# Attention scores of two heads in one pass over row halves of the array

## The chip, the cores and the metric

One core of one Trainium2 chip runs the whole kernel. The metric is device time in microseconds of one execution; lower is better. TensorE does matrix products into PSUM banks, VectorE (DVE) and ScalarE (ACT) read PSUM, GpSimd (POOL) works on SBUF, and SyncE (SP) issues most DMAs. The five run side by side and wait for each other by semaphores; each works through its own instructions in the order in which the program issues them.

## The reference

Three stages follow each other: attention with hashed buckets, a mixture of experts, and a mixing stage. The change touches the first one alone, for 2 batches of 8 heads, 768 positions, 64 dimensions:

```python
q_bits = (einsum('bhsd,dk->bhsk', q, proj) > 0)      # 6 bits; k_bits likewise
mask = q_bucket[:, :, :, None] == k_bucket[:, :, None, :]
scores = where(mask, q @ k.T / sqrt(64), -1e9)
attn = exp(scores - max(scores)); attn /= sum(attn) + 1e-9
out = attn @ v
```

## The kernel before

Heads are taken in 8 pairs (2 batches of 4), with the 64 dimensions of the two heads of a pair above each other in the 128 partitions. A pair has two halves of 384 queries, a half three blocks of 128, and each block a unit for each head: 96 units `u`, 6 to a group `g`, 16 groups. In what follows a pair of units is the two heads of one query block, 48 in all.

Single-precision products come from two halves of each number: a high part rounded to fp32r and the rest, a low part. A score is the sum of high x high, high x low and low x high. The bucket test is an addition too: 12 rows of bits (each bit and its complement, the keys' scaled by a huge number) add a penalty wherever a bit differs.

For each pair of heads, GpSimd makes the high and low parts (`split_hi`, `split_lo`) in the tile `hl`, and DMAs on SP's queue (`place`) lay them out anew in the operand tile `op`: for each head, 128 rows hold q high twice over k high and k low, and 76 rows hold q low and 12 rows of bits. A unit's scores (`scores`, L198) are then four matmuls over 128 columns of queries, one 128-row and one 76-row product for each half of 384 keys. They go to a buffer `ps` of two PSUM banks; there are two such buffers.

What follows a unit's scores:

- `low` (L205): one VectorE instruction takes the row minimum (signs are turned) and moves the 768 scores out of PSUM into `sc`;
- `expo` (L212): ScalarE's exponential with the row sum;
- `transp` (L226 to L232): six TensorE transposes through two banks `pst`, copied out by ScalarE or VectorE; three copies in four are ScalarE's;
- `av` (L243): attention times values in two column halves of the array, one for each head, four matmuls after every odd unit, each of which the chip runs as two instructions; `av_out` takes the result out after six;
- `av_tok` (L260 to L275): once in a group, the product with the identity and gate weights, and its small VectorE steps.

The order is written out by hand. The main loop runs over units: scores of unit u + 2, `av` after odd units, transposes of u (which also issue `low` and `expo` of u + 2), then a list of side jobs that `at` has put down for this unit: splits and placing for the next pair of heads, bits (`bit_part`: the dots of L118 on TensorE in four column groups, signs on VectorE, a GpSimd multiply), loads, and `narrow`, the conversion of 64-bit weights for the third stage (a load, three VectorE steps, L528 to L532, and a store). The first pair of heads is prepared by hand ahead of the loop: copies on ScalarE and GpSimd make head 0's operands (L424 to L431), VectorE its bits, and DMAs head 1's; six warm-up matmuls stand between. The first six units go head by head.

Of the kernel before, what the change touches and what calls it, by code (L numbers as in the profile page):

```python
# [27 lines left out]
NW = 4  # L28
C_ID, C_TRI, C_ONE = 0, 128, 256
# [29 lines left out]
def attention(tc, nc, cst, cbf, cst_src, tri_src, cw, qkT, vt, iw_src, route, wide, errands, xh, early):  # L59
    with ExitStack() as ctx:  # L60
# [24 lines left out]
        rawt, vtile, bits, opnd, hls = {}, {}, {}, {}, {}  # L85

        def load_pair(i):
            b, p = pairs[i]
            r = raw_p.tile([128, 2, S], F32, name="rqk")
            if i == 0:  # L90
                nc.sync.dma_start(r[:, 1], qkT[b, p, :, 1])
                nc.sync.dma_start(r[:, 0], qkT[b, p, :, 0])
            else:
                nc.sync.dma_start(r, qkT[b, p])
            rawt[i] = r
# [36 lines left out]
        def bits_here(s, hf, pd):  # L132
            sl, p = slice(384 * hf, 384 * hf + 384), 64 * s
            to = opnd[0][64:76, 0, 2 + s, sl]
            nc.vector.tensor_scalar(to, pd[p:p + 12, :384], 0.0, cw[p:p + 12, 32:33],
                                    op0=ALU.is_gt, op1=ALU.subtract)
            return to

        def split_hi(i, j):
            raw = rawt[i]  # L140
            if j == 0:
                hls[i] = hl_p.tile([128, 4, S], F32R, name="hl")
                if i == 0:
                    nc.scalar.activation(hls[i][:, 2], raw[:, 1], AF.Copy)
                else:
                    nc.gpsimd.tensor_scalar(hls[i][:, 2], raw[:, 1], 1.0, 0.0, op0=ALU.mult, op1=ALU.add)
            elif i == 0:
                nc.scalar.activation(hls[i][:, 0], raw[:, 0], AF.Copy, scale=-0.125)
            else:
                nc.gpsimd.tensor_scalar(raw[:, 0], raw[:, 0], -0.125, 0.0, op0=ALU.mult, op1=ALU.add)  # L150
                nc.gpsimd.tensor_scalar(hls[i][:, 0], raw[:, 0], 1.0, 0.0, op0=ALU.mult, op1=ALU.add)

        def split_lo(i, j):
            raw, hl = rawt[i], hls[i]
            if j == 0:
                eng = nc.gpsimd if i else nc.vector
                eng.tensor_tensor(hl[:, 3], raw[:, 1], hl[:, 2].bitcast(F32), op=ALU.subtract)
            elif i == 0:
                nc.vector.scalar_tensor_tensor(hl[:, 1], raw[:, 0], -0.125, hl[:, 0].bitcast(F32),
                                               op0=ALU.mult, op1=ALU.subtract)  # L160
            else:
                nc.gpsimd.tensor_tensor(hl[:, 1], raw[:, 0], hl[:, 0].bitcast(F32), op=ALU.subtract)

        def place(i, h, j):
            if i not in opnd:
                opnd[i] = op_p.tile([128, 2, 4, S], F32R, name="op")
            o32, h32 = opnd[i].bitcast(F32), hls[i].bitcast(F32)
            bt, r0 = bits[i]
            hs = slice(64 * h, 64 * h + 64)
            if j == 0:  # L170
                nc.sync.dma_start(o32[0:64, h, 1:4:2], h32[hs, 2:3].to_broadcast([64, 2, S]))
            elif j == 1:
                nc.sync.dma_start(o32[64:128, h, 0:2], h32[hs, 0:4:3])
            elif j == 2:
                nc.sync.dma_start(o32[0:64, h, 0:4:2], h32[hs, 0:2])
            else:
                for s in range(2):
                    c = r0 + 64 * s + 12 * h
                    nc.sync.dma_start(o32[64:76, h, 2 + s], bt[c:c + 12])

        units = [(i, half, qb, h) for i in range(NPR) for half in range(2) for qb in range(3) for h in range(2)]
        units[:6] = sorted(units[:6], key=lambda t: (t[3], t[2]))
# [4 lines left out]
        def scores(u):  # L187
            i, half, qb, h = units[u]
            op = opnd[i]
            g = u // 6  # L190
            if u % 6 == 0:
                sums[g] = sm_p.tile([128, 6], F32, name="sum")
                mns[g] = sm_p.tile([128, 6], F32, name="mn")
            ps = ps_s.tile([128, 2, 512], F32, name="ps")
# [5 lines left out]
            pss[u] = ps  # L200
# [14 lines left out]
        def transp(u):  # L215
# [6 lines left out]
            for n in range(2):  # L222
# [10 lines left out]
                if n == 0 and u + 2 < NU:  # L233
                    low(u + 2)
            if u + 2 < NU:
                expo(u + 2)
# [9 lines left out]
        def av_out(g, q0=0, q1=3):  # L246
            if q0 == 0:
                xTs[g] = sm_p.tile([128, 384], F32, name="xT", bufs=2)
# [44 lines left out]
        def cut(x, p0, m, eng):  # L293
            if not xcut:
                t = op_p.tile([128, 2, 4, S], F32R, name="op").rearrange("p a b s -> p (a b s)")
                for h in range(2):
                    xcut[h] = t[:, 3072 * h:3072 * h + 3072].rearrange("p (a t d) -> p a t d", a=2, t=3)
# [8 lines left out]
        def pick(ks):  # L306
            if not hot:
                t = op_p.tile([128, 2, 4, S], F32R, name="op").rearrange("p a b s -> p (a b s)")
# [27 lines left out]
        def narrow(m, j):  # L336
            src, dst = wide[m]
            if j == 0:
                w64[m] = d_p.tile([128, S], U32, name="w64", bufs=3)
# [16 lines left out]
        busy, relieve = set(), set(range(1, NU - 1, 2))  # L356
        for n in range(1, NPR):
            u0 = 12 * (n - 1)
            u1 = u0 + 3 if n == 1 else u0
            at(u1, split_hi, n, 0)  # L360
            at(u1, split_hi, n, 1)
            at(u1 + 1, split_lo, n, 0)
            at(u1 + 2, split_lo, n, 1)
            for h in range(2):
                for j in range(4):
                    at(u1 + 3 + j, place, n, h, j)
# [4 lines left out]
        for u0, ids in ((1, [1]), (9, [2, 3]), (26, [4, 5]), (50, [6, 7])):  # L371
            for hf in range(2):
                at(u0 + hf, lambda ids=ids, hf=hf: bit_part(ids, hf, px_tile))
                busy.add(u0 + hf)
# [3 lines left out]
        for m in range(len(wide)):  # L378
            for j in range(1, 4):
                x = free.pop(0)  # L380
                at(x, narrow, m, j)
                if j == 1 and m + 2 < len(wide):
                    at(x, narrow, m + 2, 0)
            at(x + 1, narrow, m, 4)
        for x, f in enumerate(errands):
# [4 lines left out]
        for x, f in zip((0, 1, 3, 4, 5, 6, 7, 8, 9), [copy] + seg):  # L390
# [4 lines left out]
        tok[70], tok[71] = [8], [9]  # L395
# [19 lines left out]
        idle = ps_a.tile([128, 512], F32, name="pav")  # L415
        warm(nc, cbf, idle, 13)
        opnd[0] = op_p.tile([128, 2, 4, S], F32R, name="op")
        op = opnd[0]
        split_hi(0, 0)
        hl = hls[0]  # L420
        split_lo(0, 0)
        split_hi(0, 1)
        for x in (1, 3):
            nc.gpsimd.tensor_scalar(op[0:64, 0, x], hl[0:64, 2], 1.0, 0.0, op0=ALU.mult, op1=ALU.add)  # L424
        pds = [bit_dots([0], hf, pt_tile) for hf in range(2)]
        warm(nc, cbf, idle, 6)
        split_lo(0, 1)
        nc.scalar.activation(op[0:64, 0, 0], hl[0:64, 0], AF.Copy)
        nc.scalar.activation(op[64:128, 0, 1], hl[0:64, 3], AF.Copy)
        nc.scalar.activation(op[64:128, 0, 0], hl[0:64, 0], AF.Copy)  # L430
        nc.scalar.activation(op[0:64, 0, 2], hl[0:64, 1], AF.Copy)  # L431
        k0 = bits_here(1, 0, pds[0])
        bits_here(0, 0, pds[0])
        nc.vector.tensor_scalar(k0, k0.bitcast(F32), -MISS, None, op0=ALU.mult)
        k1 = bits_here(1, 1, pds[1])
        nc.vector.tensor_scalar(k1, k1.bitcast(F32), -MISS, None, op0=ALU.mult)
        place(0, 1, 0)
        place(0, 1, 1)
        place(0, 1, 2)
        for hf in range(2):  # L440
            bit_signs(bits[0][0], hf, pds[hf])
        place(0, 1, 3)
        nc.sync.dma_start(op.bitcast(F32)[64:76, 0, 2, 384:], bits[0][0][0:12, 384:])
        nc.sync.dma_start(iw, iw_src)
        nc.sync.dma_start(tri, tri_src)
        load_v(0)
        load_pair(2)
        load_v(1)
        load_pair(3)
        for u in range(2):  # L450
            scores(u)
            low(u)
            expo(u)
        nc.gpsimd.tensor_copy(cbf[:, 0:128], ident)
        nc.gpsimd.tensor_copy(cbf[:, 128:384], tri)
        for u in range(NU):
            g, w = u // 6, u % 6
            last = g == NG - 1
            if u + 2 < NU:
                scores(u + 2)  # L460
            if g >= 1 and not last and w % 2 == 1:
                av(g - 1, w - 1)
                av(g - 1, w)
            if w == 5 and g >= 1 and not last:
                av_out(g - 1)
            if last and w == 1:
                for kb in range(3, NB):
# [1005 lines left out]
```

## Time and profile before

| | us |
|---|---|
| median of 3 runs | 641.53 |
| the runs | 638.04, 642.39, 641.53 |
| the profiled execution | 639.75 |
| span of its instructions | 637.9 |

| engine | busy in the span | share |
|---|---|---|
| TensorE | 621.0 | 97% |
| VectorE | 404.0 | 63% |
| ScalarE | 355.3 | 56% |
| GpSimd | 262.0 | 41% |

The profiled execution is 1.85 us longer than the span from its first to its last instruction; the rest lies around it. Busy shares are means over three stages; attention fills the first 250 us or so. TensorE counts as busy from the start of a matmul to its modelled end, and neighbours overlap, so the durations of single matmuls don't add up to the time that a stream takes.

### The profile page before, as it was taken

The numbers are of one execution on the slowest core, as the hardware profiler recorded it, in microseconds if no ns is written. First come the engines' busy times: TensorE is split into PE (matmuls) and PEld (weight loads), VectorE is DVE, ScalarE is ACT, GpSimd is POOL, SyncE is SP. The second block draws the span as 40 slices with busy tenths as digits, with TensorE's granted clock in tenths as the row PEclk, the third lists the DMA queues.
The fourth block names the chain that finished last, engine by engine and source line by source line (L and its number), as shares of the span: only waits on it lengthen the run. The fifth ranks groups of instructions, "written<-read, shape, count | busy, mean of one in ns | idle before, by whom it ended". The sixth has DMA issues, their size and how long they took to land. (4 is left out here: it accounts for less than half of the span.)

```text
span 637.9 us, 10353 instructions
## 1 busy us (share of the span) xinstructions
PE 621.0 (97%) x3930; PEld 501.9 (79%) x3930; DVE 404.0 (63%) x743; ACT 355.3 (56%) x645; POOL 262.0 (41%) x195
## 2 busy tenths in 40 slices
PE   7989998999999999999999999999999999999997
PEld 4746766667677677889899889989688887878897
DVE  6636768788888666846885655644356877663352
ACT  5747766767767766454555455444656546743220
POOL 2432221124080241345346354255456766684320
PEclk8979999999999999999999999999999999999999
DMA  7997999965976201688768698764222432221002
GB/s 198 265 234 203 305 260 289 260 165 159 259 219 157 74 1 50 232 294 316 272 226 312 233 308 306 256 247 168 82 85 85 145 100 84 101 97 67 33 34 100
DMA packets 52861, 116.13 MB, mean 182 GB/s; under 512 B 4180, under 2 KB 13664, under 8 KB 52808
## 3 DMA queue, kind: packets, MB, share of 16 engines
q1 hardware_dynamic: 49448, 101.28, 51.2%
q10 hardware_dynamic: 1440, 7.86, 3.6%
q0 software_dynamic: 1920, 6.29, 3.0%
q8 instruction: 32, 0.52, 0.3%
q14 instruction: 21, 0.17, 0.1%
HBM read 74.06 MB, written 22.54 MB: 151 GB/s over the span
## 5 line engine op out<-in xcount | busy, mean ns | idle before, releaser
L205 DVE TENSOR_SCALAR_CACHE_REDUCE sc<-ps 128x768 f32<-128x768 f32 x96 | 91.4, 953 | 33.2 <-PE ps L198 32.2
L1199 PE MATMUL acc<-wt,z 128*128 128x256 f32 (+1 forms) x576 | 105.4, 338 | 0.6 <-DVE z L1185 0.6
L1199 PEld LDWEIGHTS acc<-wt,z 128*128 128x128 f32 x576 | 89.8, 188 | 15.7 <-DVE z L1185 1.5
L784 POOL TENSOR_TENSOR whl<-wr,whl 128x1024 fp32r<-128x1024 f32 x30 | 72.0, 2425 | 69.6 <-ACT whl L782 69.6
L212 ACT ACTIVATE sc<-sc,mn 128x768 f32<-128x768 f32 x96 | 89.8, 936 | 18.6 <-DVE sc L205 15.4
L198 PE MATMUL ps<-op 76*128 76x384 f32 (+1 forms) x384 | 94.2, 367 | 4.8 <-DMA op<-bt 2.2
L857 PE MATMUL mph<-xhl,whl 128*128 128x256 f32 x768 | 94.2, 284 | 0.4 <-DVE xhl L520 0.3
L857 PEld LDWEIGHTS mph<-xhl,whl 128*128 128x128 f32 x768 | 93.2, 192 | 1.3 <-DVE xhl L520 0.5
L226 PEld LDWEIGHTS pst<-cst,sc 128*128 128x128 f32 x576 | 66.5, 143 | 31.7 <-ACT sc L212 18.5
L230 ACT ACTIVATE pt<-pst 128x384 f32<-128x384 f32 x143 | 65.0, 487 | 41.8 <-PE pst L226 41.5
L226 PE MATMUL pst<-cst,sc 128*128 128x128 f32 x576 | 83.6, 282 | 1.7 <-DVE pt L232 1.6
L873 PE MATMUL mpy<-whl,h 128*128 128x512 f32 x336 | 79.5, 392 | 0.0
L198 PEld LDWEIGHTS ps<-op 76*128 76x128 f32 (+1 forms) x384 | 64.5, 194 | 12.9 <-issue 5.9
L243 PE MATMUL pav<-pt,v 128*64 128x384 f32 (+1 forms) x432 | 74.2, 468 | 0.0
L782 ACT ACTIVATE whl<-wr 128x1024 fp32r<-128x1024 f32 x64 | 64.0, 1051 | 15.1 <-PE mpy L873 6.5
L873 PEld LDWEIGHTS mpy<-whl,h 128*128 128x128 f32 x336 | 62.1, 188 | 12.4
L552 POOL TENSOR_TENSOR wt<-wr,wt 128x768 fp32r<-128x768 f32 x24 | 46.2, 1946 | 10.0 <-ACT wt L551 4.6
L243 PEld LDWEIGHTS pav<-pt,v 128*64 128x64 f32 x432 | 26.4, 137 | 28.7 <-issue 28.5
L784 DVE TENSOR_TENSOR whl<-wr,whl 128x1024 fp32r<-128x1024 f32 x34 | 40.0, 1219 | 6.4 <-ACT whl L782 6.4
L860 ACT ACTIVATE h<-mph 128x512 fp32r<-128x512 f32 x32 | 19.1, 596 | 43.1 <-PE mph L857 41.6
L861 DVE SCALAR_TENSOR_TENSOR h<-mph,h 128x512 fp32r<-128x512 f32 x32 | 21.8, 689 | 33.3 <-ACT h L860 33.2
L1225 PE MATMUL bk<-u,wch 128*128 128x512 f32 (+1 forms) x192 | 34.0, 335 | 0.9 <-DVE u L1215 0.9
(186 smaller groups left out, 792.7 us busy)
## 6 DMA issues: line engine op xcount, KB each, us to landing
wr<-w SPq DMA_DIRECT2D x32, 1024.0 KB
op<-hl SPq DMA_DIRECT2D x45, 384.0 KB
wr<-wtf ACTq DMA_DIRECT2D x10, 768.0 KB
w<-wt SPq DMA_DIRECT2D x16, 384.0 KB
rqk<-qkT SPq DMA_DIRECT2D x7, 768.0 KB
xs<-wr SPq DMA_DIRECT2D x8, 512.0 KB
xi<-xs SPq DMA_DIRECT2D x7, 512.0 KB
ys<-y SPq DMA_DIRECT2D x7, 512.0 KB
```

What stands on the lines that cost most here:

```text
L198: nc.tensor.matmul(ps[:, n, :384], lhsT=op[:kk, h, x, c0:c0 + 128], rhs=op[:kk, h, x + 1, 384 * n:384 * n + 384], start=(x == 0), stop=(x ...
L205: nc.vector.tensor_scalar(sc.rearrange("p (a b) -> p a b", a=2), pss.pop(u)[:, :, :384], NEG, None, op0=ALU.min, op1=ALU.min, accum_out=mn ...
L212: nc.scalar.activation(sc, sc, AF.Exp, bias=mns[g][:, w:w + 1], scale=-1.0, accum_out=sums[g][:, w:w + 1])
L226: nc.tensor.transpose(ps[:, 128 * j:128 * j + 128], sc[:, 128 * kb:128 * kb + 128], ident)
L230: nc.scalar.activation(dst, src, AF.Copy)
L243: nc.tensor.matmul(pav[g][64 * h:64 * h + 64, sl], lhsT=vtile[g // 2][:, kb, 64 * h:64 * h + 64], rhs=pts[g][h][:, kb, sl], start=(kb == 0 ...
L552: self.nc.gpsimd.tensor_tensor(t[:, 1, r], raw[:, sl], t[:, 0, r].bitcast(F32), op=ALU.subtract)
L782: nc.scalar.activation(t[0][:, sl], raw[:, sl], AF.Copy)
L784: lo.tensor_tensor(t[1][:, sl], raw[:, sl], t[0][:, sl].bitcast(F32), op=ALU.subtract)
L857: nc.tensor.matmul(ps[:, ff], lhsT=w[a][:, w0:w0 + 128], rhs=x[:, bb, k], start=(n == 0), stop=(n == 23))
L873: nc.tensor.matmul(yps[e][n], lhsT=h[:, a, fo, 128 * n:128 * n + 128], rhs=w[bb][:, 512 * f:512 * f + 512], start=(fo == 0 and q == 0), st ...
L1199: nc.tensor.matmul(span(b, d, t0, n), lhsT=z[:, a, r, 128 * d:128 * d + 128], rhs=w[:, bb, r, t0:t0 + n], start=(t == 0 and i == 0 and (d ...
```

## The change

The operand tile and the DMAs that fill it go. Scores are taken straight from `hl`, in which the two heads of a pair already stand in partitions 0 to 63 and 64 to 127: three products of 64 rows for each head and each half of the keys, with the heads in turn, so that neighbours use different row halves of the array. The bits go to a tile `bb` of their own, four times (two heads, two halves of the keys) at partitions 0, 32, 64 and 96, and add their penalty in four matmuls of 12 rows. Both heads of a block go together: the loop runs over 48 pairs of units, and both score buffers fill at once.

`hl` gets four buffers instead of one, and the side jobs of the next pair of heads move: splits start up to a pair ahead, bits are placed five units after. The copies out of the transposes are dealt anew, again three to ScalarE and one to VectorE. `narrow` has two 64-bit buffers instead of three and loads at the end of a tile's steps instead of after the first. The first pair of heads is prepared in two halves of q; its bits are written by VectorE straight into `bb`, for which `cw` holds four more copies of the projection (163 columns instead of 33); the second warm-up goes.

The core of the diff:

```diff
-        hl_p = pool("hl", 1, side="right")
-        op_p = pool("opnd", 2, side="right")
+        hl_p = pool("hl", 4, side="right")
+        bb_p = pool("bb", 2, side="right")
-        sc_p = pool("sc", 3, left)
+        sc_p = pool("sc", 4, left)
...
+        def first_dots(x, alloc):
+            pd = alloc()
+            raw = rawt[0]
+            if x < 2:
+                nc.tensor.matmul(pd[:, :384], lhsT=cw[:, 33:161], rhs=raw[:, 0, HALF[x]], start=True, stop=True)
+                return pd
+            for r in range(4):
+                c = 32 * r
+                nc.tensor.matmul(pd[c:c + 32, :384], lhsT=cw[:, 33 + c:65 + c], rhs=raw[:, 1, HALF[r % 2]],
+                                 start=True, stop=True, tile_position=(0, c))
+            return pd
+
+        def first_signs(x, pd):
+            to = bbs[0][:, 384 * x:384 * x + 384]
+            c = 161 + x // 2
+            nc.vector.tensor_scalar(to, pd[:, :384], 0.0, cw[:, c:c + 1], op0=ALU.is_gt, op1=ALU.subtract)
+            if x == 2:
+                nc.scalar.activation(to, to.bitcast(F32), AF.Copy, scale=-MISS)
...
+        def place(i):
+            bbs[i] = bb_p.tile([128, 3 * 384], F32R, name="bb")
+            o32 = bbs[i].bitcast(F32)
             bt, r0 = bits[i]
+            for h in range(2):
+                c = r0 + 12 * h
+                for n in range(2):
+                    r = 64 * h + 32 * n
+                    nc.sync.dma_start(o32[r:r + 12, 0:S], bt[c:c + 12])
+                    nc.sync.dma_start(o32[r:r + 12, S:], bt[64 + c:76 + c, HALF[n]])
...
+        def scores(p):
+            i, half, qb, _ = units[2 * p]
+            hl, bb, g = hls[i], bbs[i], p // 3
...
+            ps = [ps_s.tile([128, 2, 512], F32, name="ps") for _ in range(2)]
             c0 = 384 * half + 128 * qb
-            for x, kk in ((0, 128), (2, 76)):
+            cols = slice(c0, c0 + 128)
+            for x, (a, bc) in enumerate(((0, 2), (0, 3), (1, 2))):
                 for n in range(2):
-                    nc.tensor.matmul(ps[:, n, :384], lhsT=op[:kk, h, x, c0:c0 + 128],
-                                     rhs=op[:kk, h, x + 1, 384 * n:384 * n + 384], start=(x == 0), stop=(x == 2))
+                    for h in range(2):
+                        hs = slice(64 * h, 64 * h + 64)
+                        nc.tensor.matmul(ps[h][:, n, :384], lhsT=hl[hs, a, cols], rhs=hl[hs, bc, HALF[n]],
+                                         start=(x == 0), stop=False)
+            for n in range(2):
+                for h in range(2):
+                    r = 64 * h + 32 * n
+                    nc.tensor.matmul(ps[h][:, n, :384], lhsT=bb[r:r + 12, cols], rhs=bb[r:r + 12, S:],
+                                     start=False, stop=True)
...
-                if n == 0 or u in relieve:
+                if n == h:
+                    if u + 2 < NU and h == 0:
+                        nc.scalar.activation(dst, src, AF.Copy)
+                        low(u + 2)
+                        continue
+                    if u + 2 < NU:
+                        expo(u + 2)
                     nc.scalar.activation(dst, src, AF.Copy)
+                elif h == 0:
+                    nc.scalar.activation(dst, src, AF.Copy)
+                    if u + 2 < NU:
+                        expo(u + 2)
                 else:
+                    if u + 2 < NU:
+                        low(u + 2)
                     nc.vector.tensor_copy(dst, src)
...
+            at(u0, split_hi, n, 0)
+            at(u0, split_lo, n, 0)
             at(u1, split_hi, n, 1)
+            at(u1, split_lo, n, 1)
+            at(u0 + 5, place, n)
...
+        nc.scalar.activation(hl[:, 2], rawt[0][:, 1], AF.Copy)
+        first_hi(0)
+        pd = first_dots(2, pt_tile)
+        nc.vector.tensor_tensor(hl[:, 3], rawt[0][:, 1], hl[:, 2].bitcast(F32), op=ALU.subtract)
+        first_signs(2, pd)
+        pd = first_dots(0, pt_tile)
+        first_lo(0)
+        first_signs(0, pd)
+        scores(0)
+        pd = first_dots(1, px_tile)
         for u in range(2):
-            scores(u)
             low(u)
             expo(u)
+        first_signs(1, pd)
...
+        for p in range(NU // 2):
+            g, w, u = p // 3, p % 3, 2 * p
             last = g == NG - 1
             if u + 2 < NU:
+                scores(p + 1)
+            transp(u)
+            if g >= 1 and not last:
+                av(g - 1, 2 * w)
+                av(g - 1, 2 * w + 1)
+                if w == 2:
+                    av_out(g - 1)
...
+            if not last:
+                transp(u + 1)
```

## Rows read from the trace of the kernel before

**Rows 1.** Windows: busy time (instructions) of each engine, granted TensorE clock, DMA share.

```profile
100.00:200.00 100.00, 99.38 (x665) 70.58 (x667) 82.92 (x200) 71.79 (x157) 26.45 (x29) 1.00 0.77 208
```

**Rows 2.** Timeline of TensorE, 216 to 224 us: start, length, instructions of a run.

```profile
218.53 0.88 PE L226 MATMUL pst<-cst,sc 128*128 128x128 f32 x6
219.16 0.95 PE L198 MATMUL ps<-op 128*128 128x384 f32 x4
219.95 0.82 PE L226 MATMUL pst<-cst,sc 128*128 128x128 f32 x6
220.53 0.95 PE L198 MATMUL ps<-op 128*128 128x384 f32 x4
221.41 1.51 PE L243 MATMUL pav<-pt,v 128*64 128x384 f32 x8
222.85 0.87 PE L226 MATMUL pst<-cst,sc 128*128 128x128 f32 x6
```

**Rows 3.** Timeline of TensorE, 168 to 171 us.

```profile
168.44 0.82 PE L226 MATMUL pst<-cst,sc 128*128 128x128 f32 x6
169.19 0.30 PE L629 MATMUL px<-cbf,erow 1*128 1x1 bf16 x6
169.42 0.96 PE L198 MATMUL ps<-op 128*128 128x384 f32 x4
```

**Rows 4.** Timeline of TensorE, 0 to 26 us.

```profile
5.53 1.50 PE L118 MATMUL pst<-rqk,cw 128*32 128x384 f32 x16
...
12.61 1.65 PE L198 MATMUL ps<-op 128*128 128x384 f32 x4 [0.91 <-DVE sc L205]
...
20.08 0.82 PE L226 MATMUL pst<-cst,sc 128*128 128x128 f32 x6
20.83 0.85 PE L118 MATMUL px<-rqk,cw 128*32 128x384 f32 x8
21.61 0.97 PE L198 MATMUL ps<-op 128*128 128x384 f32 x4
```

**Rows 5.** Groups of instructions, 100 to 200 us: busy us, mean ns, idle before.

```profile
L205 DVE TENSOR_SCALAR_CACHE_REDUCE sc<-ps 128x768 f32<-128x768 f32 x43 | 41.0, 953 | 7.1 <-PE ps L198 6.8 <-ACT sc L212 0.2
L212 ACT ACTIVATE sc<-sc,mn 128x768 f32<-128x768 f32 x43 | 40.3, 936 | 12.0 <-DVE sc L205 8.9 <-DVE X L275 3.0
...
L232 DVE COPY pt<-pst 128x384 f32<-128x384 f32 x22 | 12.1, 552 | 0.0
...
L205 DVE DVE_READ_ACCUMULATOR sc<-ps 128x1 f32 x42 | 3.5, 83 | 0.0
```

**Rows 6.** Timeline of all engines, 3 to 9 us.

```profile
4.48 0.84 ACT L144 ACTIVATE hl<-rqk 128x768 fp32r<-128x768 f32 x1 [2.49 <-DMA rqk<-qkT]
...
5.35 0.96 DVE L157 TENSOR_TENSOR hl<-rqk,hl 128x768 fp32r<-128x768 f32 x1 [4.10 <-ACT hl L144]
...
6.29 1.51 DVE L159 SCALAR_TENSOR_TENSOR hl<-rqk,hl 128x768 fp32r<-128x768 f32 x1
...
7.84 1.25 DVE L135 TENSOR_SCALAR op<-pst,cw 12x384 fp32r<-12x384 f32 x2
```

**Rows 7.** Timeline of TensorE, 26 to 50 us.

```profile
38.31 0.62 PE L198 MATMUL ps<-op 76*128 76x384 f32 x2 [2.24 <-DMA op<-bt]
...
46.40 0.96 PE L198 MATMUL ps<-op 128*128 128x384 f32 x4
```

**Rows 8.** Windows behind that wait; the clock is the last column but two.

```profile
40.00:42.00 2.00, 2.00 (x11) 1.04 (x4) 1.29 (x6) 1.03 (x2) 0.13 (x1) 0.50 1.11 338
```

**Rows 9.** DMA issues: queue, count, size of each.

```profile
op<-hl SPq DMA_DIRECT2D x45, 384.0 KB
```

**Rows 10.** Timeline of all engines, 94 to 102 us.

```profile
96.58 1.82 POOL L162 TENSOR_TENSOR hl<-rqk,hl 128x768 fp32r<-128x768 f32 x1
96.70 1.74 DVE L272 TENSOR_TENSOR L<-L,lg 128x27 f32<-128x27 f32 x1
...
100.31 0.55 PE L226 MATMUL pst<-cst,sc 128*128 128x128 f32 x3 [1.60 <-DVE pt L232]
```

More of the change, by code (lines that the diff above doesn't have):

```diff
@@ L91, in load_pair @@
                 nc.sync.dma_start(r[:, 1], qkT[b, p, :, 1])
-                nc.sync.dma_start(r[:, 0], qkT[b, p, :, 0])
+                for x in range(2):
+                    nc.sync.dma_start(r[:, 0, HALF[x]], qkT[b, p, :, 0, HALF[x]])
             else:
@@ L164, in place @@
[L164 to L167, printed above, removed]
-            bt, r0 = bits[i]
[L169 to L179, printed above, removed]
+            nc.gpsimd.tensor_tensor(hl[:, 3 - 2 * j], raw[:, 1 - j], hl[:, 2 - 2 * j].bitcast(F32), op=ALU.subtract)
@@ L354, in at @@
             todo[u].append(lambda: f(*args))
-        busy, relieve = set(), set(range(1, NU - 1, 2))
+        busy = set()
         for n in range(1, NPR):
             u0 = 12 * (n - 1)
-            u1 = u0 + 3 if n == 1 else u0
-            at(u1, split_hi, n, 0)
+            u1 = u0 + 4 if n == 1 else u0 + 1
+            at(u0, operands, n)
+            at(u0, split_hi, n, 0)
+            at(u0, split_lo, n, 0)
             at(u1, split_hi, n, 1)
[L362 to L366, printed above, removed]
+            at(u1, split_lo, n, 1)
+            at(u0 + 5, place, n)
             if n + 3 < NPR:
@@ L381, in attention @@
                 at(x, narrow, m, j)
[L382 to L383 removed]
             at(x + 1, narrow, m, 4)
+            if m + 2 < len(wide):
+                at(x + 1, narrow, m + 2, 0)
         for x, f in enumerate(errands):
@@ L414, in attention @@
         load_pair(1)
[L415 to L444, printed above, removed]
         nc.sync.dma_start(tri, tri_src)
@@ L447, in attention @@
         load_pair(2)
+        nc.sync.dma_start(iw, iw_src)
         load_v(1)
         load_pair(3)
+        idle = ps_a.tile([128, 512], F32, name="pav")
+        warm(nc, cbf, idle, 13)
+        operands(0)
+        bbs[0] = bb_p.tile([128, 3 * 384], F32R, name="bb")
+        hl = hls[0]
+        nc.scalar.activation(hl[:, 2], rawt[0][:, 1], AF.Copy)
+        first_hi(0)
+        pd = first_dots(2, pt_tile)
+        nc.vector.tensor_tensor(hl[:, 3], rawt[0][:, 1], hl[:, 2].bitcast(F32), op=ALU.subtract)
@@ L458, in attention @@
             last = g == NG - 1
             if u + 2 < NU:
[L460 to L467, printed above, removed]
+                scores(p + 1)
[5 more added lines that the diff above has]
+                    av_out(g - 1)
+            elif last and w == 0:
+                for kb in range(NB):
@@ L468, in attention @@
                     av(g - 1, kb)
                 av_out(g - 1)
-            if last and w in (2, 4):
-                q = w // 4
+            elif last:
                 for kb in range(NB):
-                    av(g, kb, q, q + 1)
-                av_out(g, q, q + 1)
-            transp(u)
-            if last and w == 0:
-                for kb in range(3):
-                    av(g - 1, kb)
-            for x in tok.get(u, ()):
-                av_tok(x)
-            for f in todo.pop(u, ()):
-                f()
+                    av(g, kb, w - 1, w)
+                av_out(g, w - 1, w)
@@ L483, in attention @@
+            if not last:
+                transp(u + 1)
+            for y in (u, u + 1):
+                if last and y > u:
+                    transp(y)
+                for x in tok.get(y, ()):
+                    av_tok(x)
+                for f in todo.pop(y, ()):
+                    f()
         for u in sorted(todo):
@@ L1441, in arrange @@
     cw[:, 32] = np.where(np.arange(128) < 64, ~first, first)
+    for r in range(4):
+        h = r // 2
+        for x in range(2):
+            k = 33 + 32 * r + 6 * x
+            cw[64 * h:64 * h + 64, k:k + 6] = inp["proj"]
+    cw[:, 161], cw[:, 162] = ~first, first
     out = {"cst": cst, "tri": tri, "cw": cw}
```

80 lines of the change are left out of this document (30 added, 50 removed).

## The prediction

> **What bounds the kernel now.** I read the windows by stage first, then the TensorE timeline of a quiet stretch, then the groups of VectorE and ScalarE. From 100 to 200 us TensorE is busy 99.38 of 100 us at clock 1.00, while VectorE has 82.92 and ScalarE 71.79 [rows 1]. Busy could hide waiting, so the next view must show that the stream is dense. In [rows 2] add start and length of each run to get its end, and subtract ends: transposes end at 219.41, the four score matmuls of a unit at 220.11, six transposes at 220.77, four scores at 221.48, eight attention-value instructions (AV) at 222.92, six transposes at 223.72. So a unit's scores take 0.70 to 0.71 us (0.177 per matmul), six transposes 0.66 (0.11 each), AV 1.44, and the transposes after AV 0.80 instead of 0.66. Nothing in that list is a wait: the pair of units takes 223.72 - 219.41 = 4.31 us, all of it matmul stream. TensorE's stream is the bound, and what the change does to it is what counts; VectorE and ScalarE matter only if the new order brings them onto its path.
>
> **The score block.** Before, a pair of units has 8 matmuls of 0.177: 1.41 us. After, it has 12 of 64 rows, alternating between the two row halves, and 4 of 12 rows in four row groups. If row groups run beside each other, this is 6 + 1 = 7 slots. That such neighbours overlap is seen here for column groups: eight AV instructions of some 0.49 us each fit into 1.44 us [rows 2], which four slots explain and eight don't. For the slot I take 0.177, the pitch of the same 384-column operands; the lower bound is 0.161, AV's pitch per pass ((1.44 - 0.15 of switching) / 8). So 7 x 0.177 = 1.24, a gain of 0.17 us a pair (0.28 at 0.161).
>
> **The switches.** The pair now goes from 128 rows to 64, to 32, and back. The trace of before has one kind of matmul with a partial row group, the one-row matmuls of L629. Their run ends at 169.49, and the four scores behind it end at 170.38 [rows 3]: 0.89 where 0.70 is the rule. The way out of a row group thus costs 0.19. On the way in, too, they start 0.75 after the six transposes began (168.44 to 169.19), where scores start 0.58 after (219.95 to 220.53 in [rows 2]). Column groups tell the same: scores after the bit dots of L118 end at 22.58, 0.90 after 21.68 [rows 4], and transposes after AV take 0.14 more [rows 2]. I therefore charge 0.19 into the 64-row block, 0.19 from 64 to 32 rows, 0.14 from there to the transposes: 0.52 a pair. The bounds are 0 (row groups that share the array freely; a switch has nothing to give) and 0.57 (0.19 each). Block: 1.24 + 0.52 = 1.76 against 1.41, **0.35 us worse a pair** (0.24 at a slot of 0.161). The pair goes from 4.31 to 4.66. The switch into AV now comes from transposes rather than scores; it stays one switch and costs nothing more.
>
> [...] No row here shows four row groups at work.
>
> **VectorE between blocks.** Both halves of a block finish together at its end, and the next block needs both score buffers back, so two evictions must fit between them. One is 0.953 + 0.083 us [rows 5], two are 2.07. TensorE has 4.66 - 1.76 = 2.90 us of transposes and AV there, so the slack is 0.83. Before, one eviction had 4.31 - 0.70 = 3.61. In the three first pairs there is no AV: the gap is 1.32, shorter than 2.07, and VectorE sets the pace at 1.76 + 2.07 + some 0.07 of wake-up = 3.9 a pair. The copies out of the transposes (0.552 on VectorE, the rest on ScalarE, with exponentials of 0.936 [rows 5]) keep their number and division. ScalarE has 71.79 us for 43 units, 3.3 a pair: no bound. Score buffer sc goes from 3 to 4, which the pairs need; I price it at nothing.
>
> **The start.** Removed are the copies into the operand tile (four on ScalarE, two on GpSimd), the second warm-up, and the DMAs for head 1. By rows: the high part of k starts at 4.48 [rows 6], with the wider cw and one more DMA issue ahead of it 4.8, and ends 5.65. VectorE then has the low part of k, 0.96, to 6.6; a sign step of 0.62 (half of the 1.25), to 7.2; the low part of half of q, 0.75 (half of 1.51, which had GpSimd beside it), to 8.0; the signs of q, to 8.6. TensorE is ready earlier (half of its run of 1.50 from 5.53 [rows 4], then the q dots), so the first block ends near 9.1. Two evictions: 11.2 for the second block, then 15.1, 19.0 plus two sign steps of 0.62 (20.2), 24.1, and with AV 28.8. Then a bit part each (21.68 - 20.90 = 0.78 [rows 4]; its way out is in the block): 34.2, and pair 7 begins at 39.7. Before it begins at 46.40 [rows 7]: **6.7 us gained**. They come out of the late start; out of the wait of 2.24 us for the bits' DMA at 38.31; and out of the half clock that follows it (0.50 from 40 to 42 [rows 8]) and shows at 12.61 too (four scores in 1.65 us, not 0.97 [rows 4]). The bits of pair 1 now leave 2.5 pairs ahead of use, not one unit, and without the operands in front of them, so I take the wait as gone. Bounds: 1.5, if the idle 0.8 us a pair in the VectorE-paced pairs (3.9 - 1.76 - 1.32) bring the half clock again, and 8.
>
> **DMA and other queues.** 45 transfers of 384 KB for the operands vanish [rows 9], 17 MB; eight small ones a pair (36 and 18 KB) replace six large and four small on SP's queue, so SP issues less. TensorE waited for DMA once to any effect, which is counted above. The splits on GpSimd move up to a pair earlier into four buffers; their number stays, and nobody waits for them (a whole pair of slack, 26 us; uncovered, some 6 us of splits a pair). The place step waits for the bits' GpSimd multiply on SP; behind it stand loads needed pairs later. The narrowing of wide weights has two 64-bit buffers instead of three, and its load is issued three units ahead, some 7 us, instead of five: 0, and up to 3 us if loads come late, as VectorE would then wait with an eviction behind it. From the end of attention on, matmuls are unchanged and dense, so a shift of attention shifts the end.
>
> **The sum** against the profiled execution's 639.75: -6.7 at the start, and 41 pairs (7 to 47) x 0.35 = +14.4: 647.4, so **647.5**. The profiled time lies 1.8 under the median of the runs, 641.53, and inside their range; one per cent, about what a measurement of this kernel can tell from none, is 635.1 to 647.9.
>
> **Rivals.** *Row groups switch for free.* For it: L629 is a single place, with bf16 weights, and only its way out is cleanly seen. Against: column groups show the same 0.19. Then the block is 1.24, each pair gains 0.17, and the time is 639.75 - 6.7 - 7.0 = 626; with one of three switches paid, 634. This is the other side: **faster**. It decides from a switching cost under 0.17 a pair plus what the start gives.
> *VectorE ends the slack.* Eight VectorE instructions last over 1.3 us between 95 and 231 us, each beside a GpSimd tensor_tensor, as at 96.70 beside 96.58; two in a row made TensorE idle 1.60 us at 100.31 [rows 10], with 3.61 us of room. With 0.83 each could cost 1 to 1.5, and the token steps some 0.3 in 13 pairs: 8 to 16 more, 656 to 664. Against: most small steps fall under the next block's 1.76.
> *Weight loads of the halves don't overlap.* 16 loads at the 0.11 that a transposing matmul with its own load needs make slots of 0.22, and 0.44 for the bits: 6 x 0.04 + 0.26 = 0.5 a pair over 48 pairs, 671. AV's column halves speak against it.
> *The halves don't run together* and the change does not do what it says: 16 x 0.177 = 2.83, 1.59 more a pair, 724.
>
> **Chances.** Forecast 0.52 (own range 641 to 656: down, the slot at 0.161 takes 4.5 and the start's better bound 1.3; up, its worse bound adds 5.2 and late loads 3); free switches 0.20; VectorE 0.15; loads 0.08; no overlap 0.05. The range 628 to 664 leaves out the last two and the edge of the second. Faster by over 1%: nearly all of the free switches and a little of the forecast, 0.22. Within: half of the forecast and the rest, 0.31. Slower: 0.47.
>
> **What would show it.** In the changed kernel's TensorE timeline, ends from the last transpose to the last bit matmul should differ by some 1.6, and the transposes behind take 0.80; a 64-row pair of matmuls should start within some 10 ns and follow at 0.18. Pair 7's scores should begin near 40 us and attention's last scores some 7.7 us later than now. No wait for the bits' DMA; clock 1.00 from 30 us on. I am wrong if the block takes 1.3 (free switches), if evictions are what blocks wait for after the third pair (VectorE), or if matmuls of the two heads come one after the other.

## The result, and the profile after

The kernel after takes **648.15 us** (median of 4 runs, 647.16 to 648.41); the kernel before took 639.79 beside it (4 runs, 638.04 to 642.39). The ratio is 1.0124 [1.0079, 1.017]: slower by some 8 us. The profiled executions agree: 647.95 us with a span of 645.8, against 639.75 and 637.9. The medians and ratios of the experiments leave out two executions over 1.5% above the fastest of their kernel: one of `start_early` and one of the kernel before, on the chip of `sums_five` and `start_only_five`.

First the quiet stretch, the timeline of TensorE of the kernel after (start, length, instructions of a run), which answers to [rows 2]:

```profile
219.63 0.88 PE L239 MATMUL pst<-cst,sc 128*128 128x128 f32 x6
220.44 1.32 PE L205 MATMUL ps<-hl 64*128 64x384 f32 x12
221.68 0.45 PE L210 MATMUL ps<-bb 12*128 12x384 f32 x4
222.06 0.88 PE L239 MATMUL pst<-cst,sc 128*128 128x128 f32 x6
222.87 1.51 PE L264 MATMUL pav<-pt,v 128*64 128x384 f32 x8
224.31 0.88 PE L239 MATMUL pst<-cst,sc 128*128 128x128 f32 x6
```

Read the ends (start and length): transposes 220.51, the twelve 64-row matmuls 221.76, the four 12-row matmuls 222.13, transposes 222.94, AV 224.38, transposes 225.19. So the 64-row part takes 1.25, the bits 0.37, the transposes behind them 0.81 instead of 0.66. From the transposes ahead of one block to those ahead of the next it is 225.19 - 220.51 = 4.68 us a pair, all matmul stream, where [rows 2] gave 4.31: **+0.37 a pair**. In the single records of this block the matmuls of the two row halves start within 5 ns of each other, and those of one half end some 0.175 apart. Twelve matmuls in 1.25 us are thus six slots and one switch (6 x 0.175 + 0.19): the two halves ran beside each other.

Then the start. The timeline of TensorE again, after, against [rows 4, 7]:

```profile
6.54 1.39 PE L205 MATMUL ps<-hl 64*128 64x384 f32 x12
7.93 0.45 PE L210 MATMUL ps<-bb 12*128 12x384 f32 x4
...
9.45 0.44 PE L205 MATMUL ps<-hl 64*128 64x384 f32 x1 [0.22 <-DVE sc L218]
10.32 1.32 PE L205 MATMUL ps<-hl 64*128 64x384 f32 x11 [0.44 <-DVE sc L218]
...
13.09 0.93 PE L239 MATMUL pst<-cst,sc 128*128 128x128 f32 x6 [0.25 <-ACT pt L244]
13.94 0.85 PE L120 MATMUL px<-rqk,cw 128*32 128x384 f32 x8
...
32.17 0.85 PE L120 MATMUL px<-rqk,cw 128*32 128x384 f32 x8
32.95 1.31 PE L205 MATMUL ps<-hl 64*128 64x384 f32 x12
...
38.41 1.31 PE L205 MATMUL ps<-hl 64*128 64x384 f32 x12
```

Pair 7's scores begin at 38.41, not at 46.40 [rows 7]: **8.0 us gained**. No wait for a DMA stands on the way, and the windows show no half clock there, where [rows 8] had 0.50. But the windows do show a fall of the clock much later, in a stretch where the kernel before kept 1.00 [rows 1] (busy time and instructions of PE, PEld, DVE, ACT, POOL; granted clock; DMA share; GB/s):

```profile
40.00:42.00 2.00, 2.00 (x18) 1.12 (x14) 1.76 (x3) 1.38 (x3) 1.92 (x2) 1.00 0.00 0
100.00:200.00 100.00, 97.52 (x754) 61.72 (x750) 73.07 (x175) 62.93 (x142) 20.40 (x24) 0.98 0.40 125
196.00:198.00 2.00, 2.00 (x8) 0.61 (x8) 0.00 (x0) 2.00 (x4) 0.00 (x0) 0.50 0.00 0
```

From 100 to 200 us TensorE is busy 97.52 us, less than the 99.38 of [rows 1], though VectorE and ScalarE are less busy too (73.07 and 62.93 against 82.92 and 71.79). The timeline of TensorE shows where the rest is:

```profile
184.94 1.32 PE L205 MATMUL ps<-hl 64*128 64x384 f32 x12
...
190.37 1.36 PE L205 MATMUL ps<-hl 64*128 64x384 f32 x12
...
193.47 0.55 PE L239 MATMUL pst<-cst,sc 128*128 128x128 f32 x3 [1.37 <-ACT sc L225]
195.14 0.77 PE L239 MATMUL pst<-cst,sc 128*128 128x128 f32 x3 [1.12 <-ACT pt L249]
195.84 2.83 PE L264 MATMUL pav<-pt,v 128*64 128x384 f32 x8
...
200.20 1.32 PE L205 MATMUL ps<-hl 64*128 64x384 f32 x12
```

TensorE stops twice, the AV behind the stops runs at half clock (2.83 for 1.51), and the pair with its token step takes 200.20 - 190.37 = 9.83 us. The pair before it, with a token step too, takes 190.37 - 184.94 = 5.43. So **4.4 us are lost** at this one place. The releasers are ScalarE's exponential and a copy that ScalarE makes behind it; the timeline of ScalarE says for what the exponential waited:

```profile
187.54 0.48 ACT L251 ACTIVATE pt<-pst 128x384 f32<-128x384 f32 x1
192.39 0.94 ACT L225 ACTIVATE sc<-sc,mn 128x768 f32<-128x768 f32 x1 [4.37 <-DVE X L296]
```

Block starts subtracted from those of before, pair by pair, give the account. Those of pair 47, the last, are in the timelines of TensorE of before and of after:

```profile
241.66 0.96 PE L198 MATMUL ps<-op 128*128 128x384 f32 x4
249.62 1.34 PE L205 MATMUL ps<-hl 64*128 64x384 f32 x12
```

The difference is -8.0 at pair 7, -6.9 at 10, -5.8 at 13, -5.1 at 16, -5.8 at 19, -4.7 at 22, -1.0 at 37, +4.8 at 40, +8.0 at 47. It climbs by 1.1 in three quiet pairs. Between 16 and 19 it falls by 0.7 in place of that climb, 1.8 less, since before stood still for 1.60 there [rows 10] and after does not. Between 37 and 40 it jumps, at the stops above.

### The profile page after: what moved, and what is told of

The parts are those of the page before. It is cut to its first block, busy times and chain, and to the rows that moved or that the text cites. A ratio compares the mean times of both kernels' runs of the same rounds, so it can differ in the third digit from the quotient of the medians.

```text
span 645.8 us, 11075 instructions
## 1 busy us (share of the span) xinstructions
PE 630.9 (98%) x4304; PEld 493.0 (76%) x4304; DVE 400.5 (62%) x739; ACT 348.2 (54%) x644; POOL 258.2 (40%) x191
## 4 chain that ended last, share of the span: by engine, by line
PE 81%; DVE 10%; ACT 4%; issue 1%; DMA 1%; POOL 1%; ACTq 0%; DVEq 0%; POOLq 0%
PE mph L866 13%; PE pst L239 12%; PE mpy L882 11%; PE pav L264 11%; PE ps L205 9%; PE acc L1208 8%; PE bk L1234 4%; PE ps L210 3%; PE bk L1111 2%; PE px L281 2%; DVE w L539 1%; DVE s L1189 1%; DVE th L1123 1%; PE ps L352 1%; PE px L120 1%
## 5 line engine op out<-in xcount | busy, mean ns | idle before, releaser
L218 DVE TENSOR_SCALAR_CACHE_REDUCE sc<-ps 128x768 f32<-128x768 f32 x96 | 89.2, 954 | 34.8 <-PE ps L210 34.7
L239 PEld LDWEIGHTS pst<-cst,sc 128*128 128x128 f32 x576 | 61.4, 141 | 40.1 <-issue 33.2
L205 PE MATMUL ps<-hl 64*128 64x384 f32 x576 | 64.9, 353 | 0.7 <-DVE sc L218 0.7
L244 ACT ACTIVATE pt<-pst 128x384 f32<-128x384 f32 x47 | 23.0, 490 | 74.7 <-PE pst L239 74.7
L205 PEld LDWEIGHTS ps<-hl 64*128 64x128 f32 x576 | 48.7, 184 | 13.2 <-issue 4.2
L257 DVE COPY pt<-pst 128x384 f32<-128x384 f32 x48 | 26.7, 557 | 31.3 <-PE pst L239 31.3
L128 POOL TENSOR_SCALAR bt<-bt 64x384 f32<-64x384 f32 x8 | 4.1, 510 | 99.4 <-DVE bt L127 99.4
```

Source lines behind the costliest of these rows:

```text
L205: nc.tensor.matmul(ps[h][:, n, :384], lhsT=hl[hs, a, cols], rhs=hl[hs, bc, HALF[n]], start=(x == 0), stop=False)
L218: nc.vector.tensor_scalar(sc.rearrange("p (a b) -> p a b", a=2), pss.pop(u)[:, :, :384], NEG, None, op0=ALU.min, op1=ALU.min, accum_out=mn ...
L239: nc.tensor.transpose(ps[:, 128 * j:128 * j + 128], sc[:, 128 * kb:128 * kb + 128], ident)
```

## The experiments

**One more switch** (`bits_between`). The bits go between the second and the third product:

```
             for x, (a, bc) in enumerate(((0, 2), (0, 3), (1, 2))):
+                if x == 2:
+                    for n in range(2):
+                        for h in range(2):
+                            r = 64 * h + 32 * n
+                            nc.tensor.matmul(ps[h][:, n, :384], lhsT=bb[r:r + 12, cols], rhs=bb[r:r + 12, S:],
+                                             start=False, stop=False)
...
```

> The same 16 matmuls a block, only in another order: the four 12-row ones stand between the second and the third product, so the block goes 128, 64, 32, 64 rows and back, one switch more. If a change of row group costs 0.19 us (the block of the changed kernel shows 0.37 for its four bit matmuls, a slot of 0.18 and the rest), 48 x 0.19 = 9.1 us more than the changed kernel: about 657. If the 0.37 is what four row groups need for themselves and switches are free: no change, 648.

Measured: 659.35 us against 638.24, ratio 1.0347 [1.0314, 1.038]. TensorE's timeline of this run:

```profile
217.00 0.88 PE L240 MATMUL pst<-cst,sc 128*128 128x128 f32 x6
217.80 0.97 PE L211 MATMUL ps<-hl 64*128 64x384 f32 x8
218.70 0.44 PE L206 MATMUL ps<-bb 12*128 12x384 f32 x4
219.07 0.62 PE L211 MATMUL ps<-hl 64*128 64x384 f32 x4
```

The last four 64-row matmuls end 219.69 - 219.14 = 0.55 after the bits: two slots of 0.177 and 0.19 of switch. The block, 217.88 to 219.69, takes 1.81 instead of 1.62, and in quiet stretches three pairs take 0.56 to 0.58 longer than in the kernel after. The added switch of row groups thus cost another 0.19 in this block, and the expectation of no change falls. The sum over the pairs holds more than these switches: two new stops of VectorE's making (0.95 and 0.78 us, taken up with VectorE's slack below) and 2.5 us less at the stops near 193 us. The profiled execution takes 657.56, near the theory's 657 in part because these cancel; the median lies 11.2 above the kernel after, on another chip and with a mean granted clock of 0.992 in two of the four executions.

**The bits twice** (`bits_twice`). The group of four 12-row matmuls is issued twice (the bits are then added twice):

```
+            for again in range(2):
                 for n in range(2):
                     for h in range(2):
...
-                                     start=False, stop=True)
+                                     start=False, stop=(again == 1))
```

> The four bit matmuls are issued twice in a row; the penalty doubles, which leaves the masked scores masked. If the four row groups run beside each other, a second round is one slot of 0.177 without a switch: 48 x 0.18 = 8.5 us more than the changed kernel, about 656.5. If they run one after the other or the 0.37 is their own price: 0.37 to 0.7 a block, 18 to 34 us, 666 to 682.

Measured: 657.09 us, ratio 1.0309 [1.0277, 1.0341]. The eight are one run in TensorE's timeline:

```profile
218.73 1.33 PE L205 MATMUL ps<-hl 64*128 64x384 f32 x12
219.99 0.62 PE L211 MATMUL ps<-bb 12*128 12x384 f32 x8
```

0.62 for eight, 0.45 for four: the second four cost 0.17 to 0.18, one slot. So the four row groups ran beside each other here, and the 0.37 of the bits is one slot and one switch.

**One head after the other** (`head_by_head`). The same twelve matmuls, six of one head and then six of the other:

```
-            for x, (a, bc) in enumerate(((0, 2), (0, 3), (1, 2))):
-                for n in range(2):
-                    for h in range(2):
+            for h in range(2):
+                for x, (a, bc) in enumerate(((0, 2), (0, 3), (1, 2))):
+                    for n in range(2):
```

> The twelve 64-row matmuls of a block are issued head by head: six in the upper row half, then six in the lower. If neighbours overlap only because they use different row halves, only the sixth and seventh still can: 11 slots in place of 6, 5 x 0.177 = 0.885 a block and 42 us more than the changed kernel, about 690. If TensorE looks far enough ahead to bring the second head's matmuls forward, or the halves never overlapped: no change.

Measured, in a single execution: 667.48 us, +19 over the kernel after, and +0.47 a pair. That would be 22.6 over 48 pairs; some 2.8 us less are lost at the two stops, which no half clock follows in this run. TensorE's timeline:

```profile
102.45 0.88 PE L239 MATMUL pst<-cst,sc 128*128 128x128 f32 x6
103.25 1.80 PE L205 MATMUL ps<-hl 64*128 64x384 f32 x12
```

The twelve end 1.72 after the transposes (105.05 - 103.33), not 1.25 and not 2.13, an estimate for two heads in sequence (1.25 and five more slots of 0.177). Neither expectation was met: the order of issue mattered, but less than a strict sequence would have made it. In the window from 103.2 to 103.8 us the same timeline has the matmuls that begin in the block's first 0.55 us:

```profile
103.25 0.90 PE L205 MATMUL ps<-hl 64*128 64x384 f32 x4
```

They are four. In the kernel after, the first 0.55 us of the block at 220.44 hold six, three of each row half. At that pace the first head alone begins three, so at least one of the four is, by this estimate, the second head's, whose first is issued after the first head's sixth. Why no more of them began so early is not shown.

**Narrowing out of the way** (`quiet_72_75`, `quiet_68_71`). First theory for the stops near 193 us: a narrowing of wide weights on VectorE, slow beside GpSimd (2.06 us at 186.22 in the kernel after, beside a GpSimd instruction of 1.81 at 186.06; the median of its line is 0.55). In each of two kernels four units get no narrowing, 72 to 75 as here, or 68 to 71:

```
-        busy = set()
+        busy = set(range(72, 76))
```

> The changed kernel, but no weight narrowing is put on units 72 to 75, where GpSimd splits the last pair of heads; the narrowing steps behind move down by up to three units. In the changed kernel a narrowing step of 2.06 us beside a GpSimd tensor_tensor at 186 us put the evictions late, and TensorE lost some 4.8 us between 190 and 200, half clock included. If VectorE's late step is the cause: about 643, and no half clock behind 190. If it was a late DMA or the blocks themselves: no change, 648. Where another pair's splits now meet a narrowing step, a new stall may eat a part.

> As quiet_72_75, aimed anew: in the changed kernel GpSimd's splits of the pair of heads that meets the late narrowing step ran at 182 to 188 us, behind scatters, beside the side jobs of units 68 to 71, so leaving units 72 to 75 free took nothing away. Here units 68 to 71 have no narrowing. If VectorE's late step beside GpSimd is the cause, the 4 to 5 us lost between 190 and 200 go: about 643.5 (the last 64-row block some 4 us earlier than the changed kernel's 249.6). If the evictions stay late for another reason (the token steps of that group, the exponentials on ScalarE): no change, 648.

Measured: 647.65, ratio 1.0167 [1.0134, 1.0201], and 649.62, ratio 1.0162 [1.013, 1.0193]. No gain, and the stops are still there. TensorE in `quiet_72_75` (in `quiet_68_71` at 200.39 and 202.05):

```profile
194.51 0.55 PE L239 MATMUL pst<-cst,sc 128*128 128x128 f32 x3 [1.39 <-ACT sc L225]
196.18 0.55 PE L239 MATMUL pst<-cst,sc 128*128 128x128 f32 x3 [1.12 <-ACT pt L249]
```

That theory falls. In both runs ScalarE's exponential still waits for the X step of L296, 4.36 and 3.66 us.

**A fifth sums buffer** (`sums_five`). The exponential of group 12 adds its row sums into a tile from a pool of four, so it takes the buffer of group 8. Group 8's token step is late (it is put at unit 71, where the rule of most groups would give 61), and its X step still reads that buffer.

```
-        sm_p = pool("sm", 4, side="right")
+        sm_p = pool("sm", 5, side="right")
```

> The kernel after with one edit: the pool of the small tiles of sums and row minima has 5 buffers in place of 4. In the kernel after, ScalarE's first exponential of group 12 waited 4.37 us for VectorE's X step of group 8's late token step, which still reads the sums tile whose buffer group 12 takes; TensorE then stood twice (1.80 and 1.39 us between 193 and 197 us), and 2 us ran at a granted clock of 0.50. Theory (the shared buffer makes the stall): with a fifth buffer that wait has nothing to wait for, the two stops and the half clock are gone, and 3.5 to 4.8 us come back: 643.5 to 644.7 against 648.15 for the kernel after, still slower than or level with the kernel before. Rival (VectorE itself is late there, and the buffer only shows it): the stops stay in the trace with another releaser, and the time is 647 to 649.

Measured: 645.82 against 640.73, ratio 1.0082 [1.0055, 1.0109], over the 643.5 to 644.7 of the theory; span 643.0, no half clock, no stop near 193, but one of 0.93 us further ahead:

```profile
183.52 0.84 PE L239 MATMUL pst<-cst,sc 128*128 128x128 f32 x6 [0.93 <-DVE pt L257]
```

The kernel before ran at 640.73 beside it and not at 639.79, so the two were run together once more, the kernel after unedited (`after_beside`) and this one (`sums_five_beside`).

> The kernel after, unedited, on one chip with the same kernel with five sums buffers. Both theories: 647 to 649, with ScalarE's wait of some 4 us for VectorE's X step before group 12's first exponential, two TensorE stops behind it and a stretch of half clock.

> The kernel after with five sums buffers, beside the kernel after on one chip. Theory (the shared buffer costs what the trace showed when the wait went, 4.3 us between the two blocks around it, less what new stops take back, 1.6 us in the one profile): 2.5 to 4.5 us less than the kernel after. Rival (the first comparison was only a difference of chips): within 1 us of it.

Measured: 648.12 (6 runs, 646.71 to 649.59) and 644.04 (6 runs, 643.23 to 644.69), ratios 1.0164 [1.0131, 1.0197] and 1.0093 [1.0062, 1.0124]: **4.1 us less**. TensorE in `after_beside`:

```profile
191.19 1.34 PE L205 MATMUL ps<-hl 64*128 64x384 f32 x12
...
194.26 0.55 PE L239 MATMUL pst<-cst,sc 128*128 128x128 f32 x3 [1.36 <-ACT sc L225]
195.93 0.55 PE L239 MATMUL pst<-cst,sc 128*128 128x128 f32 x3 [1.12 <-ACT pt L249]
196.41 1.51 PE L264 MATMUL pav<-pt,v 128*64 128x384 f32 x8
...
199.40 1.34 PE L205 MATMUL ps<-hl 64*128 64x384 f32 x12
```

and in `sums_five_beside`:

```profile
190.99 1.39 PE L205 MATMUL ps<-hl 64*128 64x384 f32 x12
...
196.49 1.31 PE L205 MATMUL ps<-hl 64*128 64x384 f32 x12
```

From block to block it is 8.21 us with four buffers and 5.50 with five. The shared buffer is the cause of the stops; that VectorE was merely late would have left them. The stops themselves are thus 2.7 us. The profiled execution of the kernel after took 9.83 over the same pair, 1.6 more, with the half clock behind the stops.

**The new start alone** (`start_only`). The first pair of heads, six pairs of units, works as in the kernel after; from unit 10 on the loop is that of before, and its scores, from unit 12 on, take operands laid out as there:

```
+        for p in range(5):
+            g, w, u = p // 3, p % 3, 2 * p
+            block(p + 1)
+            transp(u)
+            if g >= 1:
+                av(g - 1, 2 * w)
+                av(g - 1, 2 * w + 1)
+            transp(u + 1)
...
-        for u in range(NU):
+        for u in range(10, NU):
```

> The start of the changed kernel with the steady state of the one before: the first pair of heads is prepared in halves, its six blocks are taken in row halves with the bits in four row groups; its parts live in the operand tile's second buffer, and the second pair's operands are placed some 15 us ahead of use. From unit 12 on, scores, order and side jobs are those of the kernel before. If the changed kernel's gain (8.0 us by the seventh pair of units) is the start and the absent wait for the bits' DMA, and its loss the switches of the 40 blocks behind, this keeps the gain and has not the loss: 639.8 - 8 = 632 (630 to 634). If the gain came from the operands' DMA traffic or from the pairwise order in the steady state: 638 to 640.

Measured: **634.52 us** against 638.29 (12 runs, 632.96 to 637.91), ratio 0.9942 [0.9918, 0.9966]: it beats the kernel before, but by half of what the start gained in the kernel after, and misses the 630 to 634 of the theory. TensorE's timeline says why only half:

```profile
11.36 1.32 PE L226 MATMUL ps<-op 64*128 64x384 f32 x11 [0.44 <-DVE sc L239]
...
36.98 0.59 PE L209 MATMUL ps<-op 76*128 76x384 f32 x2 [2.36 <-DMA op<-bt]
...
41.88 0.44 PE L209 MATMUL ps<-op 128*128 128x384 f32 x1
```

The wait for the bits' DMA is back with 2.36 us (2.24 in [rows 7]), and pair 7 begins at 41.88: 4.5 earlier than before, not 8.0. Of the 3.5 that lack, that wait is 2.4; 1.0 is there from the second block on (11.36, not 10.32).

**The start with earlier placing** (`start_early`). `start_only`, with the bits, splits and DMAs of the second pair of heads issued some units earlier:

```
-                    at(2, place, n, h, 0)
+                at(1, lambda: bit_part([1], 0, px_tile))
+                at(1, lambda: bit_part([1], 1, pt_tile))
...
-                        at(5, place, n, h, j)
+                        at(2, place, n, h, j)
```

> start_only, in which TensorE still waited 2.36 us at 37 us for the second pair's operand DMAs, with both bit parts of that pair, its splits and its placing brought forward (bits after unit 1, placing after unit 2, the bits' four small DMAs ahead of the last operand ones). If that wait is what start_only lacked against 632: 2 to 2.4 us less than start_only, 0.990 of the kernel before. If the DMAs are late because the queue is full with first loads, or the earlier splits now hold up VectorE at the start: no change or up to 1 us more.

Measured: 636.82 against 639.80 (11 runs, 633.92 to 642.70), ratio 0.9953 [0.9924, 0.9982], no better. TensorE still stands ahead of that pair's first scores:

```profile
35.65 0.93 PE L209 MATMUL ps<-op 128*128 128x384 f32 x4 [2.00 <-issue]
```

The profile names no releaser ("issue"), so that the wait is again for the operand tile is argued and not shown. In the kernel after there are no operands to bring, and the wait is gone: some 2.4 of its 8.0 us.

**The fifth buffer with the new start alone** (`start_only_five`). The edit of `sums_five` in `start_only`:

> The kernel with the changed start alone (634.52 us), with the same fifth buffer. In the kernel before the same exponential of group 12 waited some 3 us for the same X step, but TensorE lost nothing by it, as VectorE and ScalarE had 3.61 us of room a pair. Theory: no gain, 634 to 635. Rival (the wait costs something here too): 1 to 3 us less, 631.5 to 633.5.

Measured: 638.84 against 640.73, ratio 0.9945 [0.9916, 0.9975]: the same as without it, within the intervals. With 3.61 us of room a pair for the evictions, the wait for the buffer cost TensorE next to nothing. In the timeline of the kernel before, pair 37 takes

```profile
191.40 0.96 PE L198 MATMUL ps<-op 128*128 128x384 f32 x4
...
196.84 0.96 PE L198 MATMUL ps<-op 128*128 128x384 f32 x4
```

5.44 us, where a quiet pair with a token step takes 5.05: at most 0.4.

## Why the prediction was right, and where it was off

The forecast was 647.5 us, the median is 648.15, the profiled execution 647.95. Step by step:

- **The score block** was sized right: 1.76 us predicted, 1.62 to the last bit and 0.15 behind it measured, 1.77; the pair 4.68 instead of 4.66. Seven slots and three switches cost what [rows 2, 3] had priced, and the experiments with a moved and a doubled bit group give each price by itself: 0.19 a switch, 0.18 a slot of four row groups. The rival of free switches falls, and so do the ones in which loads or halves do not overlap.
- **41 pairs x 0.35** gave +14.4. Counted over the 40 steps from pair 7 to 47, it is 40 x 0.37 = +14.8. Not counted was that a bit step ahead of a block pays the switch in the kernel before too: the scores behind it took 0.90 instead of 0.70 [rows 4], and after they take 34.26 - 33.02 = 1.24, as behind transposes. From pair 14 to 16, with two bit steps, the difference grew by 0.30 and not by 2 x 0.37. With the bit steps and route steps of all these pairs this is an estimated 1.2 us (six or seven x 0.19) that the change did not cost.
- **The start** was mis-sized: -6.7 against -8.0. The first block begins at 6.54 and ends at 8.38 (predicted 9.1), so its chain of splits and signs took less than charged. Then the pace was mis-sized the other way: I had the first pairs paced by VectorE at 3.9 us, but the bit step of 0.85 stands beside no wait and ScalarE's copies hold the second transposes for 0.25, so those pairs took 4.4 (the blocks that begin at 10.32, 14.73 and 19.14). Half clock and DMA wait are gone, as predicted.
- **VectorE's slack.** In the quiet stretch 0.83 us of room was enough: no block there waits for an eviction. Behind the start two blocks did, by some 0.7 us together, as TensorE's timeline shows; 1.32 is the rule:

```profile
155.51 1.72 PE L205 MATMUL ps<-hl 64*128 64x384 f32 x12
...
160.86 1.60 PE L205 MATMUL ps<-hl 64*128 64x384 f32 x12
```

The forecast left the term at nothing, and that failed in the main at one place, by 4.4 us. The rival named VectorE as late beside GpSimd, with 8 to 16 us in many places. That rival is real, but in the kernel after it hardly came up: of the eight long VectorE instructions that it counted (seven of them beside a GpSimd tensor_tensor, the one at 183.68 beside tensor_scalar), the attention stage of the kernel after has one, 2.06 us at 186.22. `bits_between` shows what one costs with this room, in the timelines of GpSimd, VectorE and TensorE:

```profile
53.37 1.82 POOL L163 TENSOR_TENSOR hl<-rqk,hl 128x768 fp32r<-128x768 f32 x1
53.46 1.76 DVE L274 TENSOR_SCALAR sum<-sum 128x6 f32<-128x6 f32 x1
56.38 0.98 PE L211 MATMUL ps<-hl 64*128 64x384 f32 x7 [0.50 <-DVE sc L219]
```

The step on the row sums took 1.76 us, beside the GpSimd instruction, where in the kernel after the same step took 0.42. The eviction behind it came late, and pair 10 grew by 1.14 instead of 0.19: 0.95 for one such meeting. That the kernel after has few of them is the moved side jobs and some luck, and no merit of the forecast, which left the term at nothing. What the runs show in place of the rival's many places is one, and its cause is a buffer: `av_tok` of group 8 reads a sums tile whose place group 12 needs. The wait was there before ([rows 5]: 3.0 us of ScalarE idle behind the X step), and cost at most 0.4 us with the old room.

- **A stop of before that went away.** The 1.60 us of [rows 10] was listed as a warning; it cost before 1.8 us that after does not have.

The sum from pair 7 on: -8.0 + 14.8 - 1.2 - 1.8 + 4.4 = +8.2, where the block starts show +8.0 at pair 47 and the profiled times +8.2. Not in this sum are the 0.7 of the two blocks and some 0.7 that only the kernel before lost, in pairs 24 and 25; they cancel. So the forecast came close partly by luck: an unpredicted 4.4 stood against three unpredicted gains of 4.3 (1.3, 1.2 and 1.8). Without the stops the kernel after takes 644.04, still 0.9% slower than before. The 4.4 itself holds for an execution with half clock behind the stops; in medians it is 4.1.

From the end of attention on, the shift was kept: the dense matmul stages behind it end some 8 us later as well.

## What to carry to other kernels

Before splitting a matmul's rows into independent halves, set the slots saved against the switches of row groups that come with it: here it was one slot in eight (0.18) against three switches (0.52), and the split did not pay. Where an engine's room between two bursts shrinks, as here from 3.6 to 0.8 us, look through every pool whose oldest tile a late reader still holds: here a wait that cost at most 0.4 us before ended on the path and cost 4.1. And take apart a change with two effects: the new start alone was worth 3.8 us, while in the kernel after the slower pairs ate the start's 8.0 us and some 8 more.

## What was not expected of the hardware

- In `head_by_head` the twelve matmuls, issued six and six, took 1.72 us, where two sequences would take an estimated 2.13, and four of them began in the block's first 0.55 us, where one row half of the kernel after begins three. The description of the cores ahead of the prediction has each engine work in the order of issue; for TensorE these figures speak against it.
- The same two stops were followed by half clock in some executions and not in others: the kernel after had clock 0.50 from 196 to 198 us in its profiled run, `after_beside` 1.00 behind the same stops (AV 1.51, not 2.83). Three timed executions of `after_beside` with a mean granted clock of 0.995 to 0.997 took 648.69 to 649.59 us, three with 1.000 took 646.71 to 647.54.
- A wait of 2.36 us in `start_only` left the clock at 1.00, where 2.24 in the kernel before was followed by 0.50 [rows 8]. The windows of `after_beside` and of `start_only` behind their stops (the clock is the last column but two):

```profile
196.00:198.00 2.00, 2.00 (x12) 0.88 (x13) 0.00 (x0) 1.75 (x5) 0.00 (x0) 1.00 0.00 0
40.00:42.00 2.00, 2.00 (x19) 0.92 (x16) 0.32 (x2) 1.59 (x4) 0.00 (x0) 1.00 0.36 139
```

- Two profiled executions, of `quiet_68_71` (655.57 us, the longest of its five) and of `start_only_five` (641.96), have one more stop, of 2.36 us before 181.92 and of 1.71 before 179.69, for which the profile names no releaser; its cause stays open.
